# Turning phi_q into tiles of its own, and turning the last averages and the first dense rows with VectorE through DRAM

## The chip, the cores and the metric

The kernel runs on one core of a Trainium2 chip. A core has TensorE (PE, matrix products into PSUM), VectorE (DVE), ScalarE (ACT), GpSimd (POOL) and SyncE (SP), which here only issues transfers, in order; 16 DMA engines carry them. The metric is the device time of one execution in microseconds; the figure for the kernel before is the median of 3 runs.

## The reference

Two layers, each an attention block and a dense block with residuals. With x of shape 2048 x 640 and 32 heads of 20:

```python
def _A_ref(x, wqkv, w_phi, wo):
    q, k, v = qkv[0], qkv[1], qkv[2]
    pq = jnp.einsum("bhsd,hdf->bhsf", q, w_phi)
    pk = jnp.einsum("bhsd,hdf->bhsf", k, w_phi)
    phi_q = jnp.concatenate([_softmax(pq, axis=-1), _softmax(-pq, axis=-1)], axis=-1)
    phi_k = jnp.concatenate([_softmax(pk, axis=-1), _softmax(-pk, axis=-1)], axis=-1)
    kv = jnp.einsum("bhsf,bhsd->bhfd", phi_k, v)
    z  = jnp.einsum("bhsf->bhf", phi_k)
    num = jnp.einsum("bhqf,bhfd->bhqd", phi_q, kv)
    den = jnp.einsum("bhqf,bhf->bhq", phi_q, z)[..., None] + 1e-6
    o = num / den
    return (lambda x, *d: x.transpose(*d))(o, 0, 2, 1, 3).reshape(B, S, D) @ wo

def _B_ref(x, w1, b1, w2):
    h = jnp.einsum("bsd,df->bsf", x, w1) + b1
    sp = jnp.log1p(jnp.exp(-jnp.abs(h))) + jnp.where(h > 0, h, jnp.zeros_like(h))
    act = h * jnp.tanh(sp)
    return jnp.einsum("bsf,fd->bsd", act, w2)
```

Each is applied to a layer norm of x and added to x: attention, dense, attention, dense.

## The kernel before

The 2048 rows are 8 blocks (NB) of 256 rows, each two tiles (BT) of 128. Matrix products with the weights are done three times in a shortened float32, as high part times high part and the two mixed products, so most of PE's work comes in threes ("h" and "l" tiles). A product needs its left operand with the contracted dimension on the partitions: the class `Transposed` (L265) makes such a pair of high and low tiles, either from rows that PE turns (`rows`, the transposes at L280) or from tiles that are turned already (`cols`); ACT writes the high part and DVE the low part (L286).

A layer has three stages.

**First attention stage** (`attend_first`, L387). For each block there are six steps, k0, k1, v0, v1, q0, q1: a projection on PE (L344), then for keys and queries `features` (L355): copy, maximum and minimum, subtraction, exponential, sums and division, spread over ACT, DVE and POOL and over the following steps (`pending`, `advance`). Keys meet values in L416, which sums over all rows into `kva` and `kvz`. Query features (phi_q, 1280 columns: 32 heads x two softmaxes x 20) are turned by DVE in place in blocks of 32 x 32 (L425) and stored by four transfers per tile to `e_d` (L429), in runs of 32 numbers. The query tile, one of two, is free again when these have landed. Layer 0 fetches x (L384) and normalizes it here; layer 1 reads rows that the dense stage has turned and stored (`n2_d`, `load_turned` L319). Apart from a written-out SP order at the start, a scheduler lays out the engines' instructions here.

**Second attention stage** (`attend_second`, L553). The order of PE and SP is written out by hand. `load` (L521) brings the phi_q of a block back in two "big" tiles of five groups of 120 features and a small one; the tag "big" has 5 buffers, shared with the keys of the first stage and with dense temporaries. `average` (L563) multiplies the groups by the block-diagonal `kvb` (L573) and divides (L582 to L586) into row tiles, of which there are 4. In the loop over blocks (L637) the rows of the next block's averages are turned by PE (`Transposed(rows.pop(b + 1)).all()`, L658), while the block itself is projected by `o_ws` in halves (`Rows.half`, L600) and added to x (L603). `averages(b + 2)` (L660) and `phi(b + 4)` (L661) run for b from 2 to 5, so block 7's averages are made at b = 5. x has two buffers ("x"): each block is fetched one block ahead (L646) and stored (L669) at its end, so that a fetch waits for a store. Weights of the dense stage come in between (`fetches`, `makes`), and `tail` advances the last query tiles, which the first stage leaves over. At b = 5 `fetch_next` reads the first dense block's x1, at b = 6 `begin_next` normalizes it, and at b = 7 `ahead.all()` turns it on PE.

**Dense stage** (`dense`, L681). Per block six pairs of `hidden` (L695), `mish` and, two steps later, `contract` (L737). Rows of later blocks are normalized here, turned by DVE (`spill_turned`, L311) and stored to `n1_d` or, for the next layer, `n2_d`.

Of the kernel before, what the change touches and what calls it, by code (L numbers as in the profile page):

```python
# [24 lines left out]
BT = 2  # L25
# [17 lines left out]
def kernel(  # L43
# [36 lines left out]

    def row_block(t, b):
        return t[b * BLK:(b + 1) * BLK, :].rearrange("(p t) d -> p t d", t=BT)
# [182 lines left out]
    class Transposed:  # L265
# [5 lines left out]
        def step(self):  # L271
# [13 lines left out]
            act(hi, ps[:, :n], AF.Copy)  # L285
            nc.vector.tensor_tensor(lo, ps[:, :n], hi.bitcast(F32), op=ALU.subtract)  # L286
# [24 lines left out]
    def spill_turned(rows, dst):  # L311

        dst = dst.rearrange("(j f) (t q s) -> t q f j s", f=32, t=BT, s=32)
        for t in range(BT):
            nc.vector.transpose(rows[t], rows[t])
            for q in range(4):
                nc.sync.dma_start(dst[t, q], rows[t][32 * q:32 * q + 32].rearrange("f (j s) -> f j s", s=32))

    def load_turned(src, tiles):  # L319
# [6 lines left out]
        return Transposed(cols=cols)  # L326

# [59 lines left out]
    def attend_first(layer, x_src, first):  # L387


        def fetch_normed(b):  # L390
            if layer:
                return load_turned(n2_d[b], [row_tile] * 3)
            xt = fetch(x_src, b)
# [3 lines left out]
        pending = []  # L397

# [22 lines left out]
        def queries(xts, i, ps=None):  # L421
# [3 lines left out]
            nc.vector.transpose(e, e)  # L425
            b, t = divmod(i, BT)
            dst = e_d[b].rearrange("(j f) (t q s) -> t q f j s", f=32, t=BT, s=32)
            for q in range(4):
                nc.sync.dma_start(dst[t, q], e[32 * q:32 * q + 32].rearrange("f (j s) -> f j s", s=32))  # L429
                if b == NB - 1:  # L430
                    yield

# [88 lines left out]
    def load(b):  # L521

        ta, tb, tc_ = big_tile(), big_tile(), pair_tile(F32)
        for t, g0 in ((ta, 0), (tb, 5)):

            src = e_d[b][120 * g0:120 * (g0 + 4) + P]
            src = bass.AP(tensor=src.tensor, offset=src.offset, ap=[[BLK, P], [120 * BLK, 5], [1, BLK]])
            nc.sync.dma_start(t.rearrange("f (g s) -> f g s", s=BLK), src)
        nc.sync.dma_start(tc_[:80, 0], e_d[b][1200:])
        return [(ta, tb)[g // 5][:, (g % 5) * BLK:(g % 5 + 1) * BLK] for g in range(10)] + [tc_[:, 0]]  # L530

    def finish_kv(kva, kvz, mask):

        acc, acz = row_tile(), row_tile()
        for src, dst, p1, n, w in ((kva, acc, P, 4, 120), (kvz, acz, P, 1, 120), (kvz, acz, 42, 1, 80)):
            c = 120 if w == 80 else 0
# [362 lines left out]
```

## Time and profile before

| | |
|---|---|
| median of 3 runs | 1398.32 us (1397.06 to 1398.65) |
| the profiled execution | 1396.09 us |
| its span, first to last instruction | 1394.3 us |
| granted TensorE clock | 0.999 |
| first attention stage, layer 1 | 760 to 940 us, roughly |
| second attention stage, layer 1 | 945 to 1052 us |
| transfers | 169.57 MB in 350035 packets, 286866 of them under 512 B |
| stores of phi_q | 128 issues of 160 KB, 4.0 us to landing (median) |
| loads of phi_q | 32 of 640 KB (6.6 us) and 16 of 80 KB (6.3 us) |

In rows of groups the columns are line, engine, operation, output and input, shape, number, then busy us, mean ns of one, idle time of the engine before them and what ended it. In the timeline: start us, length us, engine, line, operation, number. In lists of waits: total us, times, longest.

### The profile page before, as it was taken

The page shows a single profiled execution, that of the slowest core. Times are in us where ns is not written, and L with a number is a line of the kernel's source. Part 1 is how long each engine was busy: PE and PEld are TensorE (multiplying, and loading weights), DVE is VectorE, ACT ScalarE, POOL GpSimd, SP SyncE. Part 2 cuts the span into 40 slices and gives each one's busy share as a digit, 9 for nine tenths or more (in the row PEclk, how much of TensorE's full clock was granted, in tenths as well). Part 3 has the DMA queues.
Part 4 walks back from the last instruction along what each step waited for, and adds up shares of the span by engine and source line. Part 5 has one row for each costly group of instructions (what it writes and reads, how often), then busy time and mean ns, then how long its engine had stood idle before and what let it go on. Part 6 is the DMA issues. An engine that isn't in the chain of part 4 may idle for free. (4 is left out here: it accounts for less than half of the span.)

```text
span 1394.3 us, 28137 instructions
## 1 busy us (share of the span) xinstructions
PE 1380.7 (99%) x11528; PEld 1367.0 (98%) x11528; DVE 1075.5 (77%) x1820; ACT 583.3 (42%) x973; POOL 440.0 (32%) x334
## 2 busy tenths in 40 slices
PE   7999999999999999999999999999999999999998
PEld 7999999999999999999999999999999999999998
DVE  5797877796698877788769988888767876777775
ACT  4444433321355454545454333332235444444443
POOL 1353443343422221222234434343342211211112
PEclk9999999999999999999999999999999999999999
DMA  8533333689633432343474333357976212333200
GB/s 328 162 79 54 67 52 58 184 228 307 235 86 95 114 84 62 83 114 95 122 261 87 71 57 58 65 107 231 288 257 200 76 25 72 95 95 95 75 22 20
DMA packets 350035, 169.57 MB, mean 122 GB/s; under 512 B 286866, under 2 KB 323458, under 8 KB 349906
## 3 DMA queue, kind: packets, MB, share of 16 engines
q1 hardware_dynamic: 349906, 167.78, 44.2%
q8 instruction: 90, 1.47, 0.4%
q14 instruction: 39, 0.32, 0.1%
HBM read 104.82 MB, written 62.91 MB: 120 GB/s over the span
## 5 line engine op out<-in xcount | busy, mean ns | idle before, releaser
L737 PE MATMUL mm<-r2h,ol 128*128 128x320 f32 x1280 | 304.7, 309 | 0.0
L721 POOL TENSOR_TENSOR ol<-big,ol 128x512 fp32r<-128x512 f32 (+1 forms) x98 | 129.8, 1324 | 483.5 <-ACT ol L720 407.3
L695 PE MATMUL one<-xtl,r1h 128*128 128x256 f32 x960 | 268.2, 279 | 0.0
L695 PE MATMUL one<-xth,r1l 128*128 128x256 f32 x960 | 268.0, 279 | 0.0
L695 PE MATMUL one<-xth,r1h 128*128 128x256 f32 x960 | 265.9, 279 | 0.0
L737 PEld LDWEIGHTS mm<-r2h,ol 128*128 128x128 f32 x1280 | 219.1, 188 | 0.0
L737 PE MATMUL mm<-r2l,ol 128*128 128x320 f32 x640 | 197.3, 309 | 0.0
L344 PE MATMUL mm<-r1h,xth 128*128 128x320 f32 x600 | 187.3, 312 | 0.0
L344 PE MATMUL mm<-r1h,xtl 128*128 128x320 f32 x600 | 186.0, 310 | 0.7 <-DVE xtl L286 0.7
L344 PE MATMUL mm<-r1l,xth 128*128 128x320 f32 x600 | 186.0, 310 | 0.0
L695 PEld LDWEIGHTS one<-xtl,r1h 128*128 128x128 f32 x960 | 180.4, 188 | 0.0
L695 PEld LDWEIGHTS one<-xth,r1l 128*128 128x128 f32 x960 | 180.4, 188 | 0.0
L695 PEld LDWEIGHTS one<-xth,r1h 128*128 128x128 f32 x960 | 179.6, 188 | 0.0
L710 DVE TENSOR_SCALAR big<-big 128x512 f32<-128x512 f32 (+1 forms) x98 | 57.1, 583 | 109.9 <-ACT big L708 109.7
L379 POOL TENSOR_TENSOR r<-r,r 128x1280 f32<-128x1280 f32 x32 | 75.8, 2368 | 163.1 <-DVE r L378 157.3
L737 PEld LDWEIGHTS mm<-r2l,ol 128*128 128x128 f32 x640 | 120.2, 188 | 0.0
L712 ACT ACTIVATE big<-big,two 128x512 f32<-128x512 f32 (+1 forms) x98 | 70.1, 715 | 116.2 <-DVE big L711 116.1
L708 ACT ACTIVATE big<-one,b1s 128x256 f32<-128x256 f32 x192 | 80.8, 467 | 90.1 <-PE one L695 89.6
L720 ACT ACTIVATE ol<-big 128x512 fp32r<-128x512 f32 (+1 forms) x98 | 61.0, 622 | 136.0 <-DVE big L719 135.9
L344 PEld LDWEIGHTS mm<-r1h,xth 128*128 128x128 f32 x600 | 112.8, 188 | 1.3
L344 PEld LDWEIGHTS mm<-r1h,xtl 128*128 128x128 f32 x600 | 112.7, 188 | 1.3 <-DVE xtl L286 1.0
L344 PEld LDWEIGHTS mm<-r1l,xth 128*128 128x128 f32 x600 | 112.8, 188 | 0.1
(129 smaller groups left out, 3156.1 us busy)
## 6 DMA issues: line engine op xcount, KB each, us to landing
e_d<-r SPq DMA_DIRECT2D x128, 160.0 KB, 4.0
big<-e_d SPq DMA_DIRECT2D x32, 640.0 KB, 6.6
x_d<-xt SPq DMA_DIRECT2D x23, 640.0 KB, 3.9
xt<-x_d SPq DMA_DIRECT2D x22, 640.0 KB, 4.3
n_d<-xn SPq DMA_DIRECT2D x176, 80.0 KB, 2.1
xt<-in_x SPq DMA_DIRECT2D x16, 640.0 KB, 5.9
xn<-x_d SPq DMA_DIRECT2D x28, 320.0 KB, 4.2
v<-n_d SPq DMA_DIRECT2D x30, 256.0 KB, 3.3
```

The source lines that it names most:

```text
L344: nc.tensor.matmul(ps[:, :HC], a[:, sl], r, start=(k == 0 and n == 0), stop=(k == KD - 1 and n == 2))
L379: nc.gpsimd.tensor_tensor(eg, eg, r.unsqueeze(2).to_broadcast([P, 2 * H, DH]), op=ALU.mult)
L695: nc.tensor.matmul(ph[:, j, :], l, r, start=(n == 0), stop=(n == 3 * KD - 1))
L708: exps[0] = nc.scalar.activation(part(ta, 0)[:, j - js.start], ph[:, j, :], AF.Exp, bias=b1s[:, 2 * pr + j:2 * pr + j + 1]).ins
L710: nc.vector.tensor_scalar_min(e, e, E_CAP)
L712: nc.scalar.activation(r, n, AF.Ln, bias=two)
L720: nc.scalar.activation(ah[:, js], n, AF.Copy)
L721: nc.gpsimd.tensor_tensor(al[:, js], n, ah[:, js].bitcast(F32), op=ALU.subtract)
L737: nc.tensor.matmul(pys[t][:, c, :HC], l[:, j, sl], r, start=(f == 0 and n == 0), stop=(f == KF - 1 and n == 2))
```

## The change

It has three parts, and a few adjustments that they need.

1. phi_q of blocks 0 to 6. DVE no longer turns a query tile in place: three transposes write two "big" tiles (groups 0 to 4 and 5 to 9, with an overlap) and a small one, which collect both tiles of a block. After the second tile twelve transfers store them to `e_d` and `f_d`, whose rows are as `load` wants them, so that `load` is three plain copies. Block 7 keeps the old way, through `g_d`. Since blocks of 32 x 32 end up in another order of rows, block rows are dealt to the tiles differently: layer 0 fetches a block of x in four transfers (`fetch_parts`), and the last dense stage's store of `n2_d` uses a permuted order (`first_stage`). The last group has 96 features, with zeros.
2. Averages of blocks 6 and 7. They are made at b = 3 and b = 4, a block sooner; DVE turns their rows (`turn_blocks`) into a "big" tile, eight transfers store it to `o_d` (`spill_blocks`) ahead of the block's x, and one transfer loads it back at b = 4 and b = 5 (`load_blocks`). PE does not turn these blocks any more.
3. The first dense block's rows. x1 is fetched at b = 4, normalized at b = 5, turned by DVE and stored to `n1_d`, and loaded at b = 6; at b = 7 only the high and low parts are made.

```diff
+    def row_parts(t, b):
+        return t[b * BLK:(b + 1) * BLK, :].rearrange("(h t s u) d -> u h s t d", h=2, t=BT, u=2)
...
-    e_d = [dram.tile([EW, BLK], F32, name=f"e_d{b}") for b in range(NB)]
+    e_d = [dram.tile([2, P, EW], F32, name=f"e_d{b}") for b in range(NB - 1)]
+    f_d = [dram.tile([96, BLK], F32, name=f"f_d{b}") for b in range(NB - 1)]
+    g_d = dram.tile([EW, BLK], F32, name="g_d")
+    o_d = [dram.tile([P, BT * D], F32, name=f"o_d{b}") for b in range(NB)]
...
+    def turn_blocks(o, t, dst):
+        nc.vector.transpose(dst[:, t * D:(t + 1) * D].rearrange("p (q c s) -> p q c s", q=4, c=KD),
+                            o.rearrange("p (c q f) -> p q c f", q=4, c=KD))
+
+    def spill_blocks(src, dst):
+        dst = dst.rearrange("(q f) (t k x) -> t k f q x", q=4, t=BT, k=4)
+        for t in range(BT):
+            for k in range(4):
+                nc.sync.dma_start(dst[t, k], src[32 * k:32 * k + 32, t * D:(t + 1) * D].rearrange("f (q x) -> f q x", q=4))
+
+    def load_blocks(src):
+        cols = big_tile()
+        nc.sync.dma_start(cols, src)
+        cols = cols.rearrange("p (a c s) -> p c a s", c=KD, s=32)
+        return Transposed(cols=[cols[:, c:min(c + 2, KD)] for c in range(0, KD, 2)])
...
+        def fetch_parts(b):
+            xt = x_tile()
+            for q in range(4):
+                nc.sync.dma_start(xt[32 * q:32 * q + 32], row_parts(x_src, b)[q // 2, q % 2])
+            return xt
...
-            nc.vector.transpose(e, e)
             b, t = divmod(i, BT)
-            dst = e_d[b].rearrange("(j f) (t q s) -> t q f j s", f=32, t=BT, s=32)
-            for q in range(4):
-                nc.sync.dma_start(dst[t, q], e[32 * q:32 * q + 32].rearrange("f (j s) -> f j s", s=32))
+            if b == NB - 1:
...
+            if t == 0:
+                blocks[b] = [big_tile(), big_tile(), pair_tile(F32).rearrange("p j s -> p (j s)")[:, :192]]
+            for c, dst in enumerate(blocks[b]):
+                src = e[:, EW - 96:].rearrange("p (j f) -> p j f", f=32)
+                if c < 2:
+                    src = e[:, 600 * c:600 * c + 600]
+                    src = bass.AP(tensor=src.tensor, offset=src.offset, ap=[src.ap[0], [32, 4], [120, 5], [1, 32]])
+                    dst = dst.rearrange("p (m g t s) -> p t m g s", m=4, t=BT, s=32)[:, t]
+                else:
+                    dst = dst.rearrange("p (j t s) -> p t j s", t=BT, s=32)[:, t]
+                nc.vector.transpose(dst, src)
+            if t == BT - 1:
+                for q in range(4):
+                    qs = slice(32 * q, 32 * q + 32)
+                    for c, (src, dst, m) in enumerate(zip(blocks[b], (e_d[b][0], e_d[b][1], f_d[b]), (4, 4, 3))):
+                        nc.sync.dma_start(dst.rearrange("(m f) (q x) -> q f m x", m=m, q=4)[q],
+                                          src[qs].rearrange("f (m x) -> f m x", m=m))
...
+            for c, t in enumerate((ta, tb)):
+                nc.sync.dma_start(t, e_d[b][c])
+            nc.sync.dma_start(tc_, f_d[b])
...
+                if b == NB - 2:
+                    ahead = load_next()
                 if b in (1, 2):
                     phi(b + 3)
-                if b == NB - 3:
+                if b == NB - 4:
                     fetch_next()
+                if b in (NB - 4, NB - 3):
+                    cols[b + 2] = load_blocks(o_d[b + 2])
                 r0.half(1, one_tile())
                 mv0 = r0.mean()
-                if b == NB - 2:
-                    ahead = begin_next()
+                if b == NB - 3:
+                    spill_next = begin_next()
...
-                    nxt = Transposed(rows.pop(b + 1)).all()
+                    nxt = (cols.pop(b + 1) if b + 1 in cols else Transposed(rows.pop(b + 1))).all()
                 if 2 <= b < NB - 2:
-                    averages(b + 2)
-                    phi(b + 4)
+                    if b < NB - 4:
+                        averages(b + 2)
+                        phi(b + 4)
+                    if b == NB - 4:
+                        turned = averages_turned(NB - 1)
                 if b == 2:
                     tail()
                 if b >= 2:
                     r1.half(0, one_tile())
+                if b == NB - 5:
+                    turned = averages_turned(NB - 2)
                 r1.half(1, one_tile())
                 norm_scale(b, [mv0, r1.mean()])
+                if turned is not None:
+                    spill_blocks(turned, o_d[b + 3])
+                    turned = None
+                if b == NB - 3:
+                    spill_next()
                 xt = xs.pop(b)
                 nc.sync.dma_start(row_block(x_dst, b), xt)
...
             def begin_dense():
-                return normed(0, x1t[0])
+                rows = [row_tile() for _ in range(BT)]
+                normalize(0, rows, [x1t[0][:, t, :] for t in range(BT)])
+                return lambda: spill_turned(rows, n1_d[0])
+
+            def load_dense():
+                return load_turned(n1_d[0], (v_tile, v_tile, row_tile))
```

More of the change, by code (lines that the diff above doesn't have):

```diff
@@ L397, in attend_first @@
         pending = []
+        blocks = {}
         def advance():
@@ L631, in averages, with averages_turned @@
                     average(b, t)
+            def averages_turned(b):
+                averages(b)
+                dst = big_tile()
+                for t, o in enumerate(rows.pop(b)):
+                    turn_blocks(o, t, dst)
+                return dst
             def phi(b):
```

58 lines of the change are left out of this document (35 added, 23 removed).

## The prediction

> **What bounds the kernel now.** I read the page's busy times first, then TensorE's (PE's) list of waits, then its timeline around the transposes, then VectorE's (DVE's) groups and stage windows, and last SyncE's (SP's) timeline, because the change moves most of its work there.
>
> ```profile
> PE 1380.7 (99%) x11528; PEld 1367.0 (98%) x11528; DVE 1075.5 (77%) x1820; ACT 583.3 (42%) x973; POOL 440.0 (32%) x334
> PE mm L237 <- DMA raw<-in_wqk_t: 7.1, 3, 4.1
> PE mm L573 <- PE mm L573: 0.9, 2, 0.4
> PE mm L344 <- DVE xtl L286: 0.7, 1, 0.7
> PE one L416 <- POOL big L379: 0.3, 1, 0.3
> ```
>
> PE is busy for 1380.7 of 1394.3 us. Of the 13.6 idle, 7.1 wait for the first weights, about 4.2 lie behind the last matmul, and everything in between is 1.9. So a microsecond of PE work taken out is a microsecond gained, as long as no new wait opens; nothing that other engines save counts.
>
> ```profile
> L280 PE MATMUL one<-ident,xn 128*128 128x128 f32 x260 | 37.2, 279 | 0.0
> 998.32 1.25 PE L280 MATMUL one<-ident,xn 128*128 128x128 f32 x10
> 999.50 1.39 PE L573 MATMUL mm<-kvb,big 120*64 120x63 f32 x40
> ```
>
> A mean of 279 ns is the length of one pipelined matmul. What a transpose occupies is the distance to the next start: ten begin at 998.32 and the next work at 999.50, so 1.18 us for ten, 118 ns each.
>
> **Removed from PE.** The turns of blocks 6 and 7 of the averages and of the first dense block's rows go: 3 x 10 transposes in each of 2 layers, 60 x 0.118 = **-7.1 us**. The averages themselves are only moved (two per block, 2.7 us); 96 in place of 80 contraction rows in the last group leaves the columns streamed as they were, so I count nothing, as for the one added small clear (0.06 us, by the row of the clear at L89) before the masks.
>
> **phi_q's turn on DVE (28 tiles).**
>
> ```profile
> L425 DVE STREAM_TRANSPOSE r<-r 128x1280 f32<-128x1280 f32 x32 | 47.7, 1490 | 3.6 <-POOL r L379 3.4
> L315 DVE STREAM_TRANSPOSE xn<-xn 128x640 f32<-128x640 f32 x44 | 36.3, 834 | 2.0 <-ACT xn L116 1.9
> L286 DVE TENSOR_TENSOR xtl<-xn,xth 128x512 fp32r<-128x512 f32 x14 | 16.6, 1188 | 0.0
> 197.20:226.30 29.10, 29.10 (x228) 28.77 (x227) 21.59 (x26) 11.83 (x17) 11.75 (x6) 1.00 0.28 42
> 864.30:893.40 29.10, 29.10 (x226) 28.79 (x225) 24.81 (x28) 10.53 (x15) 12.16 (x6) 1.00 0.36 60
> ```
>
> From the first two rows a turn costs (1490 - 834)/640 = 1.025 ns per column and 178 ns fixed. One instruction of 1280 columns becomes three of 640, 640 and 96: 834 + 834 + 276 = 1944 ns, +0.45 us per tile, +0.9 per block. No row shows a turn with strided blocks. Lower bound: if the fixed part is hidden, 1376 x 1.025 = 1.41 us, a gain of 0.08. Upper bound: the dearest DVE row per column, the third above, 2.32 ns, gives 3.19 us, +1.7 per tile. I take +0.45, since it is the same operation in runs of 32. The windows are one block of the first attention stage in each layer (total, PE, weight loads, DVE): DVE is busy 21.6 of 29.1 us in layer 0 and 24.8 in layer 1, so 4.3 us are free at the tightest and even the upper bound's 3.4 fits. Counted 0. If the cover were gone, each block would grow by what exceeds it. That e is now free after the turn and not after its store also takes away waits of ACT (37.5 us in all on e_d<-r), which PE never felt: 0.
>
> **SP and the transfers.** A block's phi_q is stored by 12 issues with runs of 1280 and 256 B, where there were 8 with runs of 128 B (median issue 0.65 us); by the 0.33 us of a 128-run load (L384) that is 4 us instead of 5. Its load has 128 runs of 5 KB per tile instead of 640 of 1 KB. SP has a gap of some 15 us in each block here (from 857.4 to 872.7, for one), so 0.
>
> **The head.** Block 0 of x comes in four transfers: SP's 0.43 us becomes 1.7, and the weights that PE awaits at 10.37 us (the last part of its 7.1) are issued 1.3 us later. Between 2.4 and 5.2 us the DMA engines were about 90% full, so bytes and not issue set the landing. Bounds 0 and 1.3; I take **+0.4**. The Trainium skill, "SBUF — State Buffer", section "Door 1: The DMA port swizzle", has 32 partitions reach 8 of 16 ports, 189 against 328 GB/s; were the four quarters run one after another, 655 KB would take 3.5 instead of 2.0 us, an estimate of +1.5 by which the sum would be 1.1 worse. Nothing here shows it: the four can run side by side.
>
> **The start of the second stage.** This is the one place where I expect a price. "big" has five buffers.
>
> ```profile
> 922.50 0.36 SPq L528 DMA_DIRECT2D big<-e_d  x1
> 943.84 0.38 SPq L528 DMA_DIRECT2D big<-e_d  x1
> 946.27 4.41 SPq L528 DMA_DIRECT2D big<-e_d  x2
> 942.40 2.54 PE L416 MATMUL one<-big,v 128*64 128x120 f32 x44
> 948.18 1.03 PE L573 MATMUL mm<-kvb,big 120*64 120x63 f32 x28
> ```
>
> Before, block 0's two tiles and one of block 1 were on their way by 922.5, and block 1's second went out at 943.84, for a first average at 948.18. After, block 6's phi_q holds two buffers from its first turn (929) until its 12 stores have landed (turned 938.5, 4 us of issue, 3 of landing: 946), and the last two key tiles hold two until L416 ends at 944.9. One buffer is left. If the loads take the free buffers first, as before, the turn waits instead, a 5 us delay that reaches PE hardly: 0. If not, three tiles of 640 KB go out from 945.5; with 2.1 us for the shortest landing in the DMA table and 0.36 MB/us (360 GB/s, as the later slices of this stretch show) the third lands at 953.1, or 954.5 by the longest landing here (8.5), against 951.5 wanted: 1.6 to 3 us. Bounds 0 and 3 per layer; I take 1.0, nearer to the early order that the trace shows: **+2.0** in two layers.
>
> **The moved averages and the way through DRAM.** I re-laid layer 1's timeline from 999.5 by the old pieces: a half of a row tile 2.2 us (60 matmuls for four in 8.8), a block's averages 2.7, ten transposes 1.2. Then averages 5 end at 1002.3, 6 at 1007.2, 7 at 1017.7; block 6 begins at 1030.9, 7 at 1039.7, dense at 1048.5. Block 6's average now starts 2.2 us after block 5's. DVE frees an accumulator pair in 0.173 + 0.153 + 0.352 + 0.657 + 0.315 = 1.65 us, and did so by 1002.7 and 1004.2; PE wants them at 1004.5 and 1005.8. Block 7's phi_q, loaded at 1008.39 (landing 5.3, so 1013.7 and a little), is wanted at 1015. Margins of 1 to 2 us, counted 0; without them up to 1 us each. The way back for block 7, from the average's end at 1017.7: DVE 1.65 + 2 x 0.83, 8 stores x 0.36, landing 2.1 to 4, load 4.3 to 6.6, split 2: about 1034 to 1036, wanted 1039.7. Block 6, by the same steps from 1007.2, has 5 us to spare. The dense rows: normalized 1029.4, turned 1031, 8 stores x 0.55 (L317's 4.37 for 8) to 1035.5; behind them on SP wait block 5's store and with it, two x buffers only, the fetch of x block 7 (store 3.2, fetch 4.3: landed at about 1043, wanted 1041.9, which delays DVE but finds four accumulators free), then the load: 1044, split by 1046, wanted by the first dense matmul at 1048.5. Counted 0, smallest margin 2.5 us.
>
> **Sum:** -7.1 + 0.4 + 2.0 = **-4.7 us**. Profiled execution 1396.09 (span 1394.3 and 1.8 around it) becomes 1391.4; its distance of 2.2 to the median of 1398.32 is kept: **1393.6**.
>
> **Rivals.**
> 1. *Late loads eat the gain.* The start of the second stage at its upper bound in both layers: -7.1 + 0.4 + 6 = -0.7, 1397.6. For it: DMA engines 88% busy from 943.5 to 956. Against it: longer runs load faster. Chance 0.17.
> 2. *Slower: DVE becomes the bound of the first attention stage.* From 1.49 + 4.3/2 = 3.6 us per tile the block outgrows PE in layer 1. At three times the row's rate (4.5 us) that is 0.86 us x 14 tiles = +12, giving 1406. For it: DVE's 85% there, overlapping and strided patterns that no row shows. Against it: the linear rows. Chance 0.11.
> 3. *The turned rows come back late.* If both legs land at 8.5 us as in the saturated stretch, block 7 is about 4 us late and the dense rows 3: 7 us in each layer, 1393.6 + 14 = 1407. For it: SP's fixed order, each store held until x can be replaced. Against it: at 1025 to 1038 landings were 3 to 4 us. Chance 0.08. The Trainium skill, "VectorE: DVE Perf Modes", section "Rules for kernel authors", says to turn 128x128 on TensorE where PSUM will do, since VectorE turns only 32x32 blocks: the rule speaks against this part, and the trace does price DVE's five blocks at 834 ns against PE's 590; but PE is the bound here, and DVE not.
>
> **Numbers.** Forecast 0.64, with a range of its own of 1390 to 1395.5; rivals 0.17, 0.11, 0.08. A measurement tells about 0.2%, 2.8 us, from no change: faster 0.64, same 0.17 (rival 1), slower 0.19 (rivals 2 and 3). The range runs from 1389.5 (all 7.1 kept, and most of the 1.9 of small waits) through rival 1 to 1403, leaving out most of rivals 2 and 3.
>
> **What would show it.** PE: L280's group at 200 instead of 260, and no new row among its waits but about 1 us per layer on the phi_q load. DVE: turns of 640 columns near 0.83 us; blocks of the first stage still 29.1 us long. A longer block there means rival 2; a wait of PE on xtl at the last two blocks or at the first dense matmul means rival 3; several us of wait at the first two averages, rival 1. I am wrong if the first stage's order shifts so that PE waits where it never did.

## The result, and the profile after

The changed kernel takes 1416.68 us (median of 4 runs, 1414.67 to 1417.5) beside 1398.20 for the kernel before (4 runs): a ratio of 1.0131, 95% interval 1.0114 to 1.0149. It is slower by 18.5 us where 4.7 us of gain were forecast. The profiled execution has a span of 1415.4 us after 1394.3.

The first line is that of busy time (page, part 1); then come PE's transposes and DVE's turns of phi_q among the groups of instructions (busy time, mean ns of one, idle time before them), and PE's waits (us in total, times, longest).

```profile
PE 1384.8 (98%) x11468; PEld 1366.3 (97%) x11468; DVE 1085.2 (77%) x1890; ACT 585.5 (41%) x973; POOL 447.2 (32%) x334
```

```profile
L290 PE MATMUL one<-ident,xn 128*128 128x128 f32 x200 | 29.7, 282 | 0.0
...
L479 DVE STREAM_TRANSPOSE big<-r 128x640 f32<-128x640 f32 x56 | 43.6, 815 | 5.0 <-POOL r L408 5.0
L479 DVE STREAM_TRANSPOSE ol<-r 128x96 f32<-128x96 f32 x28 | 6.5, 234 | 0.0
```

```profile
PE mm L247 <- DMA raw<-in_wqk_t: 10.9, 3, 4.2
PE one L452 <- POOL big L408: 4.8, 2, 2.8
PE one L779 <- DVE bn L666: 2.5, 1, 2.5
PE one L779 <- ACT xth L126: 2.2, 1, 2.2
PE mm L635 <- DMA big<-e_d: 1.5, 1, 1.5
...
PE mm L373 <- ACT xth L126: 0.9, 1, 0.9
```

The 60 transposes are gone, as forecast. In their place stand waits that PE did not have: on POOL at the last keys (L452), on the rows at the first dense matmul (L779), on a phi_q load (L635); the wait for the first weights grew from 7.1 to 10.9. Where each loss arises is read best by the start of the same matmul in both traces (a projection, an average or a dense matmul):

| stretch, up to | after - before there, us | lost in it |
|---|---|---|
| first projections (30 us) | +5.0 | 5.0 |
| first stage of layer 0, block 6 | +7.7 | 2.7 |
| averages of layer 0 running | +11.7 | 3.9 |
| dense stage of layer 0 running | +15.0 | 3.4, and the 3.5 saved: 6.9 |
| first stage of layer 1, block 6 | +14.6 | -0.4 |
| averages of layer 1 running | +19.1 | 4.5 |
| dense stage of layer 1, end | +21.0 | 1.9, and the 3.5 saved: 5.4 |

The products of keys and values of block 6 stand at +8.5 and +16.1, because the scheduler puts them later among the projections; that is order and no loss. In layer 1's first stage, then, nothing was lost. Of the 2.7 us in layer 0's, 1.4 fall around block 1, at the wait of 0.9 us on ACT; the other 1.3 fall ahead of it, and of the five kernels with the same order there (this one and the first four experiments) only this one and part 1 alone have such a loss (1.3 and 1.0).

Of the first 5.0 us some 1.5 belong to the profiled execution of before, which started quickly: the ten kernels below without part 1, whose block 0 is fetched as before, stand at +1.0 to +2.2 there (mean 1.5), the five with the fetch in four parts at +4.6 to +5.5 (mean 5.0).

**The head.** Block 0 of x landed at 8.8 us before, in one transfer, and at 11.62 after, in four quarters of 32 partitions.

**DVE's cover.** These windows (total, PE, weight loads, DVE, ACT, POOL, clock, DMA share, GB/s) lie around block 1 of each layer's first stage, of the kernel before and then of after:

```profile
71.50:89.00 17.50, 17.50 (x149) 16.87 (x148) 17.50 (x24) 9.03 (x14) 10.43 (x7) 1.00 0.37 81
753.70:768.80 15.10, 14.79 (x126) 14.28 (x125) 15.10 (x13) 6.78 (x11) 7.96 (x4) 1.00 0.39 67
```

```profile
78.00:95.50 17.50, 17.50 (x147) 16.78 (x145) 17.50 (x25) 6.85 (x10) 10.48 (x9) 1.00 0.51 119
767.90:784.90 17.00, 17.00 (x141) 16.39 (x140) 17.00 (x20) 6.00 (x9) 9.34 (x5) 1.00 0.46 107
```

DVE was busy for the whole of both windows before the change already. The blocks that I had read (from 197 and 864 us) are looser. Whether this is what cost the 1.4 us is settled below, by the run on VectorE's order.

**The order at the end of the first stage.** DVE in layer 1 before, and after:

```profile
936.65 1.51 DVE L425 STREAM_TRANSPOSE r<-r 128x1280 f32<-128x1280 f32 x1 [0.61 <-POOL r L379]
938.09 1.45 DVE L377 TENSOR_REDUCE r<-big 128x64 f32<-128x1280 f32 x1
939.57 0.55 DVE L378 RECIPROCAL r<-r 128x64 f32<-128x64 f32 x1
```

```profile
949.10 1.48 DVE L406 TENSOR_REDUCE r<-big 128x64 f32<-128x1280 f32 x1
950.50 0.95 DVE L407 RECIPROCAL r<-r 128x64 f32<-128x64 f32 x2
953.58 1.57 DVE L479 STREAM_TRANSPOSE big<-r 128x640 f32<-128x640 f32 x2 [2.13 <-POOL r L408]
955.08 0.23 DVE L479 STREAM_TRANSPOSE ol<-r 128x96 f32<-128x96 f32 x1
955.24 1.45 DVE L406 TENSOR_REDUCE r<-big 128x64 f32<-128x1280 f32 x1
956.60 1.53 DVE L397 TENSOR_REDUCE m<-r 128x32 f32<-128x640 f32 x2
958.05 0.54 DVE L407 RECIPROCAL r<-r 128x64 f32<-128x64 f32 x1
```

The last key's sum (L377, now L406) is followed at once by its reciprocal before; after, the queries' reductions (L397) stand between, and the query's own reciprocal had waited for a key's sum. POOL, which multiplies by that reciprocal, starts so much later that PE waits 2.8 us for it (2.0 in layer 0). The three turns of a tile take 2 x 815 + 234 ns = 1.86 us (groups above), so their size was forecast well; the scheduler's new order was not in the sum at all.

**The end of the second stage.** SP in layer 1 after (start, time of the group, count):

```profile
1027.72 6.28 SPq L349 DMA_DIRECT2D o_d<-big  x8
...
1040.20 6.83 SPq L349 DMA_DIRECT2D o_d<-big  x8
1047.12 0.38 SPq L753 DMA_DIRECT2D x_d<-xt  x1
...
1051.68 8.01 SPq L328 DMA_DIRECT2D n_d<-xn  x8
1059.78 0.49 SPq L753 DMA_DIRECT2D x_d<-xt  x1
...
1063.50 0.33 SPq L413 DMA_DIRECT2D xt<-x_d  x1
```

Eight stores take SP 6.3 to 8.0 us where I had counted 2.9 and 4.4. In the two groups to `o_d`, 2.4 and 3.1 us of that are waiting: an issue uses the semaphore of the transfer eight issues before it again and waits until that one has landed. A store of 1031.29 went out when a phi_q load landed at 1031.28, one of 1046.72 when the load of turned rows landed at 1046.71. In the group to `n_d` only 0.3 us lie between the issues; two of the eight take 1.8 and 2.8 us themselves, and no view says why. The trace of before had such issues in a full stretch of its own, which I had not priced: four stores of phi_q in layer 1 with 0.05 us between them.

```profile
981.03 6.89 SPq L429 DMA_DIRECT2D e_d<-r  x4
```

After the change the store of x stands behind the stores of turned rows (1059.78), the fetch into its buffer behind that store (1063.50), and the load of the dense rows behind the fetch (1063.99). x is there at 1069.45 and the first dense rows at 1070.08, so block 7's residual and the split of the dense rows are late together, and PE behind both:

```profile
1067.92 0.30 PE L373 MATMUL one<-r2h,xtl 128*128 128x320 f32 x1
1070.76 0.76 PE L779 MATMUL one<-xth,r1h 128*128 128x256 f32 x2 [2.54 <-DVE bn L666]
...
1072.16 0.41 PE L779 MATMUL one<-xth,r1l 128*128 128x256 f32 x1
1072.37 0.41 PE L779 MATMUL one<-xth,r1h 128*128 128x256 f32 x1
```

The wait is followed by matmuls that start 0.21 us apart, where they start 0.117 us apart otherwise. The granted clock (third figure from the end) is 0.50 there for 3.4 us, as it is behind the wait at layer 0's first dense matmul and behind layer 1's wait on POOL, and 1.00 elsewhere behind the head:

```profile
388.16:391.57 3.41, 3.36 (x15) 3.06 (x16) 3.34 (x9) 1.51 (x3) 0.62 (x2) 0.50 1.03 411
961.60:965.01 3.41, 3.41 (x25) 3.20 (x22) 1.22 (x4) 1.27 (x1) 0.00 (x0) 0.50 0.72 258
1070.83:1074.24 3.41, 3.16 (x13) 2.86 (x14) 3.38 (x9) 1.60 (x3) 0.52 (x2) 0.50 1.04 405
```

So each of these three waits costs about 1.7 us, half of 3.4, more than its length: some 5 us of the loss.

### The profile page after: what moved, and what is told of

Its sections match the earlier page's. It is cut to its first block, busy times and chain, and to the rows that moved or that the text cites. A ratio compares the mean times of both kernels' runs of the same rounds, so it can differ in the third digit from the quotient of the medians.

```text
span 1415.4 us, 28221 instructions
## 1 busy us (share of the span) xinstructions
PE 1384.8 (98%) x11468; PEld 1366.3 (97%) x11468; DVE 1085.2 (77%) x1890; ACT 585.5 (41%) x973; POOL 447.2 (32%) x334
## 4 chain that ended last, share of the span: by engine, by line
PE 84%; DMA 6%; DVE 5%; issue 2%; ACT 1%; SPq 1%; POOL 1%; DVEq 0%; ACTq 0%; POOLq 0%
PE mm L373 25%; PE mm L821 23%; PE one L779 22%; PE one L373 7%; PE mm L635 2%; PE one L452 2%; PE one L290 1%; DMA big<-o_d 1%; DVE xtl L297 1%; DMA raw<-in_wqk_t 1%; DMA xt<-in_x 1%; DMA big<-x_d 1%; DMA big<-in_wv 1%; DMA x_d<-xt 1%; DMA xn<-in_w 0%
## 5 line engine op out<-in xcount | busy, mean ns | idle before, releaser
L779 PE MATMUL one<-xth,r1h 128*128 128x256 f32 x960 | 267.4, 281 | 4.7 <-DVE bn L666 2.5
L779 PE MATMUL one<-xtl,r1h 128*128 128x256 f32 x960 | 269.6, 281 | 0.3 <-DVE xtl L297 0.3
L779 PE MATMUL one<-xth,r1l 128*128 128x256 f32 x960 | 269.0, 280 | 0.0
L779 PEld LDWEIGHTS one<-xth,r1h 128*128 128x128 f32 x960 | 180.9, 189 | 5.4 <-ACT xth L126 5.4
L779 PEld LDWEIGHTS one<-xtl,r1h 128*128 128x128 f32 x960 | 181.7, 189 | 0.9 <-DVE xtl L297 0.9
L779 PEld LDWEIGHTS one<-xth,r1l 128*128 128x128 f32 x960 | 181.7, 189 | 0.0
```

The source lines that it names most:

```text
L779: nc.tensor.matmul(ph[:, j, :], l, r, start=(n == 0), stop=(n == 3 * KD - 1))
```

## The experiments

Times are medians beside runs of the kernel before in the same job (1397.9 to 1398.9); intervals are 95%.

**The head: one transfer.** Which rows stand in which partition changes, so the output's rows are mixed.

```diff
-            xt = x_tile()
-            for q in range(4):
-                nc.sync.dma_start(xt[32 * q:32 * q + 32], row_parts(x_src, b)[q // 2, q % 2])
-            return xt
+            return fetch(x_src, b)
```

> The changed kernel, but layer 0 fetches a block of x in one transfer of plain rows instead of four (rows of layer 0 then stand in another order than the stores assume, so the output's rows are mixed). The trace of the changed kernel puts 5 us of its loss before the first projections (30.0 to 35.1 us) and 3.3 more in the rest of layer 0's first stage. Theory (the four transfers cost it, by whatever mechanism): the first weights arrive at 10.4 again instead of 14.4, PE's waits on them go from 10.9 back to about 7.1, and the time falls by 6 to 8 us, to about 1409. Rival (the turn of phi_q on DVE and the new order cost it, the transfers only seem to): at most 2 us less, 1415 or more.

1413.77 us, ratio 1.0107 (1.0092 to 1.0122); x landed at 9.44, the first projections stand at +0.7 instead of +5.0, and 2.9 us of the median come back, between the theory's 6 to 8 and the rival's 2. The head is a cost of part 1.

**The head: four transfers of columns.** Four quarters of the columns, each over all 128 partitions (rows mixed as well).

```diff
-                nc.sync.dma_start(xt[32 * q:32 * q + 32], row_parts(x_src, b)[q // 2, q % 2])
+                cs = slice(160 * q, 160 * q + 160)
+                nc.sync.dma_start(xt[:, :, cs], row_block(x_src, b)[:, :, cs])
```

> As the run with plain x, again with rows in another order than the stores assume, but the block comes in four transfers of a quarter of the columns, each over all 128 partitions. Same bytes, same number of transfers as in the changed kernel, all partitions in each. Theory A (number: SP issues a transfer only when the one eight before it has landed, so three more transfers push the weights behind landings): the weights arrive late as in the changed kernel, PE waits 10 to 11 us for them, time within 2 us of 1416.7. Theory B (32 partitions are slow for a transfer): as with plain x, waits of 7 to 8 us, time near 1409.

x landed at 10.06 us. In the twelve kernels that fetch it in one transfer it landed between 8.8 and 10.04, in the five with quarters of 32 partitions between 11.62 and 12.41. So the number of transfers is not told from the spread, and the 32 partitions cost 1.6 us or more: the landing goes by theory B. The first projections stand at +2.4, between 0.7 and 5.0. The median (1417.63, ratio 1.0125, 1.0105 to 1.0144) doesn't show this saving.

**The store of x first.** At the end of a block of the second stage:

```diff
                 norm_scale(b, [mv0, r1.mean()])
+                xt = xs.pop(b)
+                nc.sync.dma_start(row_block(x_dst, b), xt)
...
                     spill_next()
-                xt = xs.pop(b)
-                nc.sync.dma_start(row_block(x_dst, b), xt)
```

> The changed kernel with each block's store of x ahead of the stores of turned rows on SP, at b = 3, 4 and 5. Theory (the way round SP is the price at the end of the second stage: turned rows' stores, then the store of x, then the fetch of x that DVE needs, then the load of the dense rows): stores of x go out 6 to 8 us sooner, x of block 7 lands before DVE wants it, PE's waits on the first dense matmul (2.3 and 2.7 us) shrink below 1, and the time falls by 3 to 6 us, to about 1412. Rival (the turned dense rows themselves are late, whatever the order): the waits stay or grow, since the turned rows are stored later; 1416 or more.

1420.42 us, 1.0153 (1.0129 to 1.0177). In the profile, that of the fastest execution (1415.62), the waits stay: 2.2 us at layer 1's first dense matmul on DVE bn, and in layer 0 2.0 on block 7's turned rows (ACT xth), which now come back late. My theory, that the order alone did it, fell: what stood ahead of the one stands ahead of the other.

**Part 1 alone** (phi_q in tiles of its own, x in four parts; averages and dense rows as before).

> Part 1 of the change alone: phi_q in tiles of its own with the four-part fetch of x; averages and first dense rows turned by PE as before. Theory (part 1 costs by itself: head 5, first stage of layer 0 3.3, start of the second stage 3.2 and 3.1, layer 1 1.0; parts 2 and 3 give 7.1 on PE and lose 12 at the ends of the second stages): 15 us over the kernel before, 1413 to 1414, the first dense matmul without a wait. Rival (the parts need each other: the loss at the second stage's start comes from the buffers that parts 2 and 3 hold): under 1408.

1413.54 us, 1.0113 (1.0083 to 1.0143), as its theory had it. +5.5 at the first projections, +7.8 at the end of layer 0's first stage, 3.7 and 4.5 lost at the two second stages' starts (the waits on POOL, and behind each of them 3.4 us at a granted clock of 0.50, from 278.18 and 957.43), nothing at the dense starts.

```profile
PE mm L247 <- DMA raw<-in_wqk_t: 11.4, 5, 5.0
PE one L452 <- POOL big L408: 4.8, 2, 2.8
```

**Parts 2 and 3 without part 1.** The kernel before with the moved averages, the turned blocks and the dense rows of the change; phi_q (L425, L429, L528) and x as before.

> Part 1 undone, parts 2 and 3 kept: phi_q turned in place and loaded as in the kernel before, block 6's and 7's averages and the first dense rows turned through DRAM. Theory (the loss of 12 us at the ends of the second stages is theirs alone, from 4 MB more to move per layer in a stretch whose DMA engines are full): no loss up to the first averages, then -3.5 per layer by the transposes and +5 to +7 per layer around the first dense matmul; +3 to +5 over the kernel before, 1401 to 1404, with PE waiting 2 us and more at the first dense matmul. Rival (phi_q's part crowds them, they are right by themselves): the transposes' 7 us show, 1392.

1407.78 us, 1.0073 (1.0058 to 1.0088), dearer than expected. Nothing is lost ahead of the averages; the ends of the second stages lose about 7.8 and 7.1 us, 3.5 saved in each. So both halves of the change are slower by themselves, for different reasons.

```profile
PE one L737 <- ACT xth L117: 2.4, 2, 2.0
PE one L364 <- DVE xt L623: 1.8, 2, 1.1
PE one L364 <- ACT xth L117: 1.3, 2, 0.7
PE one L737 <- DVE bn L624: 1.3, 1, 1.3
```

**Part 2 alone, part 3 alone.**

> Part 2 alone on the kernel before: averages of blocks 6 and 7 a block sooner, turned by DVE and through DRAM. It saves 40 transposes, 4.7 us. Theory (bytes in a full stretch): 2.6 MB more per layer delay the weights and x, waits of 1 to 2 us per layer at the last blocks; 1395 to 1398, near the kernel before. Rival (the first dense rows, part 3, are what is late): 1393.5.

> Part 3 alone on the kernel before: the first dense block's rows normalized a block sooner, turned by DVE, stored and loaded. It saves 20 transposes, 2.4 us. Theory (bytes in a full stretch): 1.3 MB more per layer and a chain of store, fetch of x and load that ends at the first dense matmul; waits of 1 to 3 us per layer there, 1397 to 1401. Rival (part 2 is the dear one): 1396.

1409.50 (1.0090, 1.0074 to 1.0105) and 1408.74 (1.0083, 1.0065 to 1.0102): either is as dear as both together and dearer than both of its theories, so their prices don't add. The clock has a share in that: in the profiled executions it is 0.50 for 6.8 us in each layer with part 2 alone, for 3.4 and 6.8 us with part 3 alone, and for 3.4 us in all with both. With part 3 alone, PE waits where block 7's rows are turned, for the residual sum that waits for x:

```profile
PE one L280 <- DVE xt L603: 6.9, 5, 3.4
```

**VectorE's order.** After, with the queries' reductions (L397) and the sums (L406) tied behind the previous tile's reciprocal:

```diff
+    last_recip = [None]
...
-        for s, op in ((0, ALU.max), (1, ALU.min)):
-            nc.vector.tensor_reduce(m[:, s], eh[:, 1], axis=AX.X, op=op)
+        with ExitStack() as st:
+            if last_recip[0] is not None:
+                st.enter_context(tc.issue_after(last_recip[0]))
+            for s, op in ((0, ALU.max), (1, ALU.min)):
+                nc.vector.tensor_reduce(m[:, s], eh[:, 1], axis=AX.X, op=op)
...
-        nc.vector.tensor_reduce(r, eg, axis=AX.X, op=ALU.add)
-        nc.vector.reciprocal(r, r)
+        with ExitStack() as st:
+            if last_recip[0] is not None:
+                st.enter_context(tc.issue_after(last_recip[0]))
+            nc.vector.tensor_reduce(r, eg, axis=AX.X, op=ALU.add)
+            last_recip[0] = nc.vector.reciprocal(r, r).ins
```

> The changed kernel with DVE's order in the first stage tied: the maximum, minimum and sum of a tile come no sooner than the reciprocal of the tile before. In the changed kernel's trace the reciprocal of the last query tile but two comes after a key's sum and the last key's reciprocal after two query reductions, and PE waits 2.2 and 2.9 us for GpSimd's product with it, 4 us and more per layer at the start of the second stage. Theory (the order that the scheduler laid out costs this): those waits shrink below 1 us and 4 to 7 us come back, 1410 to 1412. Rival (DVE's added work and GpSimd's lateness cost it, in any order): the waits stay, 1415 or more.

1410.13 us, 1.0094 (1.0069 to 1.012): 6.5 us come back and the waits on POOL are gone, so the order was a cause. It was also the cause of the loss around block 1 of layer 0: the five kernels with part 1 and the scheduler's order lose 1.4 to 2.0 us there, this run 0.1 (+4.6 at the first projections, +4.7 at block 6), although it makes the same three turns per tile and DVE is as full:

```profile
74.00:94.00 20.00, 20.00 (x164) 19.17 (x165) 20.00 (x28) 10.34 (x16) 13.64 (x9) 1.00 0.45 104
```

What had been hidden behind the order shows:

```profile
PE mm L642 <- DMA big<-e_d: 4.3, 3, 2.3
PE one L786 <- ACT xth L127: 3.8, 3, 2.0
```

The first are the late phi_q loads: with what follows the second stages' starts lose 3.9 us in layer 0, 1.7 of them at half clock, and 1.9 in layer 1.

**Block 6 alone through DRAM**, on the kernel before: of part 2 only what concerns `averages_turned(NB - 2)`; averages 7 stay at their old place.

```diff
-                    averages(b + 2)
-                    phi(b + 4)
+                    if b != NB - 4:
+                        averages(b + 2)
+                        phi(b + 4)
```

> One half of part 2 alone, on the kernel before: only block 6 of the averages is made a block sooner and turned through DRAM (8 stores and 1 load, 1.3 MB per layer); block 7 and the dense rows are turned by TensorE as before, phi_q and the head are as before. 20 transposes go: 20 x 0.118 = 2.4 us. Theory 'the end of the stage is what is full' (eight transfers in flight, the fetch of x block 7 behind the stores there): these 8 stores go out about 1008 to 1018, long before, and block 6 had 5 us to spare, so the gain is kept but for 0.5 us per layer: 1395 to 1397.5, waits of TensorE on xt or on split rows below 1 us. Theory 'every way through DRAM in the second stage is dear' (both blocks lost about 16 us in two layers, so half of that each): 1398.3 - 2.4 + 8 = 1404, with 2 to 4 us of wait per layer.

1401.79 us, 1.0033 (1.002 to 1.0046), over a wide spread (1398.37 to 1407.8). The 2.4 us saved aren't kept, and the theory that only the very end is full fell; the rival, at 1404, is nearer.

**Fewer transfers.** Parts 2 and 3, with four stores per turned block, and the dense rows turned into one "big" buffer too:

```diff
-        dst = dst.rearrange("(q f) (t k x) -> t k f q x", q=4, t=BT, k=4)
-        for t in range(BT):
-            for k in range(4):
-                nc.sync.dma_start(dst[t, k], src[32 * k:32 * k + 32, t * D:(t + 1) * D].rearrange("f (q x) -> f q x", q=4))
+        dst = dst.rearrange("(q f) (t k x) -> k f t q x", q=4, t=BT, k=4)
+        for k in range(4):
+            nc.sync.dma_start(dst[k], src[32 * k:32 * k + 32].rearrange("f (t q x) -> f t q x", t=BT, q=4))
...
-                return lambda: spill_turned(rows, n1_d[0])
+                flat = big_tile()
+                for t, o in enumerate(rows):
+                    turn_blocks(o, t, flat)
+                return lambda: spill_blocks(flat, n_d)
...
-                return load_turned(n1_d[0], (v_tile, v_tile, row_tile))
+                return load_blocks(n_d)
```

> Parts 2 and 3 as in the run without part 1, with the same bytes in fewer transfers: each turned block is stored by 4 issues in place of 8 (both row tiles in one transfer), and the first dense rows go the same way into one buffer (4 stores and 1 load in place of 8 and 3). 13 issues per layer at the end of the stage where there were 24 stores and 3 loads became 12 stores and 3 loads. Theory 'number' (each issue waits for the transfer eight before it, so the count of transfers sets when the fetch of x block 7 goes out): that fetch goes out some 5 us sooner, the loss per layer falls from about 7.8 to 3 or less, 1397 to 1402, and the 8 stores that took 6.3 to 8 us of SP become 4 that take under 4. Theory 'bytes' (4 MB more in a stretch whose transfers were already 0.68 to 0.99 busy): nothing changes by more than 2 us, 1406 to 1410, and 4 stores take as long as 8 did.

1401.17 us, 1.0021 (1.0013 to 1.003): 6.6 us less than with eight stores. SP in layer 1 with eight stores and with four:

```profile
1029.89 8.06 SPq L340 DMA_DIRECT2D o_d<-big  x8
...
1042.58 7.99 SPq L319 DMA_DIRECT2D n_d<-xn  x8
...
1054.40 0.33 SPq L404 DMA_DIRECT2D xt<-x_d  x1
```

```profile
1025.57 3.29 SPq L340 DMA_DIRECT2D o_d<-big  x4
...
1038.52 2.93 SPq L340 DMA_DIRECT2D n_d<-big  x4
...
1047.18 0.33 SPq L404 DMA_DIRECT2D xt<-x_d  x1
1047.67 0.33 SPq L344 DMA_DIRECT2D big<-n_d  x1
```

With four, issues of 0.58 to 1.05 us follow one another without a wait. With eight, 4.4 us of the first 8.06 are waiting for older transfers, and of the second 7.99 one issue takes 2.8 itself. The fetch of x goes out 7.2 us sooner, 3.6 of which the run with eight stores had lost before this point. The bytes are the same, so bytes are not what came back. (The dense rows also come back in one load of longer runs here; that share isn't told apart from the number.)

**The load first.** As the run with fewer transfers, and

```diff
+                if b == NB - 2:
+                    ahead = load_next()
                 if b + 1 < NB:
                     xs[b + 1] = fetch(x_src, b + 1)
-                if b == NB - 2:
-                    ahead = load_next()
```

> As the run with fewer transfers, but SyncE issues the load of the first dense rows ahead of the fetch of x block 7 instead of behind it. In that run the stores of these rows had landed at 1045.56, but the load stood behind the fetch, which waits for block 5's store of x to land and went out at 1047.18; the load followed at 1047.67 and TensorE waited about 2 us for its split at the first dense matmul, in both layers, with the clock at 0.91 for some time after. Theory 'SP's order holds the load': it goes out at about 1045.7, 2 us sooner, the wait at the first dense matmul falls below 0.5 us, and with the clock's loss after it about 2.5 us per layer come back: 1396 to 1397.5, faster than before by about 0.1%. Theory 'bytes': the load lands at the same time as before, since it shares the DMA engines with seven others, and the time stays at 1400 to 1402; or the fetch of x block 7 is now late and the wait moves to the last rows' transposes.

1398.69 us, 1.0001 (0.9992 to 1.001): about half of what was expected. The load went out at 1045.54, and PE's waits on the split dense rows (1.8 us in layer 0, 0.7 in layer 1) are gone; in their place it waits there on xt, 1.2 and 0.5 us, and 1.0 us on block 7's split rows. The expectation had misread the run that it starts from: in layer 1 that wait was 0.7 us and not 2, and the granted clock behind it was 1.00.

**The whole change with these three mended** (order, number, load first).

> The whole change (part 1 too) with three of its causes taken away: VectorE's order tied as in the run on order (6.5 us), 4 stores per turned block and the dense rows in one buffer (6.6 us in the run without part 1), and the load of these rows ahead of the fetch of x block 7 (4 us if that holds). If the causes add up: 1416.7 - 6.5 - 6.6 - 4 = 1399.6, so 1398 to 1402; what stays is the head (5), layer 0's first stage (3.3) and the late phi_q loads at both second stages' starts (2 to 4 each), against 7.1 saved. If instead block phi_q's stores and loads press on the same transfers, the second stage's end stays 3 us per layer worse than without part 1 and the time is 1403 to 1408.

1405.73 us, 1.0054 (1.0042 to 1.0066): 11 of the 17 us. The head stays (+5.4), and so do the late phi_q loads (2.8 us on big<-e_d; the starts of the second stages lose 3.5 and 3.1), and the ends of the second stages still lose 3.5 and 4.7 us. Layer 0's first stage, which the expectation had counted among what stays, loses nothing (+5.5 at block 6).

**Which way pays?** The run with the load first without block 7's part (the same edit of `averages` as for block 6 alone), and block 6 alone with four stores.

> As the run with the load first, but block 7 of the averages is turned by TensorE as before and averaged at its old place: block 6 and the first dense rows go through DRAM (4 stores and 1 load each). 40 transposes go: 40 x 0.118 = 4.7 us. In the run with the load first all three ways broke even, 7.1 saved and as much lost, and its waits stood at block 7: 1.5 us for phi_q's last load (needed a block sooner), 1.0 us for the split of its turned rows, 1.4 for the fetch of x block 7. Theory 'block 7 is the way that doesn't pay': its own 2.4 us cost 4 or more, and without it the time is 1395 to 1397 with waits below 1.5 us per layer. Rival 'what is lost goes with any transfers at the end of the stage': the dense rows' 4 stores alone still hold the fetch of x block 7, the waits stay at 2 to 3 us per layer and the time at 1398 to 1400.

> Only block 6 of the averages through DRAM, with 4 stores in place of 8 (the run with block 6 alone gave 1401.8, over a wide spread of 1398.4 to 1407.8). 20 transposes go, 2.4 us. If the count of transfers is what that run lost by, 1395.5 to 1397.5 and a spread as narrow as before's; if not, 1400 to 1402 again.

1402.42 (1.0028, 1.0018 to 1.0038) and 1401.68 (1.0021, 1.0012 to 1.0031): without block 7 both of its theories fell, and for block 6 alone the rival held: its number of stores isn't what it lost by. Fewer ways cost more than all three (1398.69), and in both PE waits for xt (6.1 and 2.0 us).

**x block 7 in a buffer of its own.** The two runs "load first" and "block 6, four stores", each with

```diff
-                    xs[b + 1] = fetch(x_src, b + 1)
+                    spare = big_tile().rearrange("p (t d) -> p t d", t=BT) if b == NB - 2 else None
+                    xs[b + 1] = fetch(x_src, b + 1, spare)
```

and in the first this fetch again ahead of the load.

> As the run with the load first, but x block 7 is fetched into a buffer of 'big' that is free by then, not into one of the two x buffers, and its fetch stands ahead of the load of the dense rows again. So it no longer waits until block 5's store of x has landed. Theory 'chain through two x buffers': add, store of x, landing, fetch two blocks on, landing, add; in the kernel before one round of it took 9.0 us (store issued 343.74, landed 347.31, fetch landed 352.79), with the turned rows' transfers ahead of it the store alone takes 7 to 10 us to land, and what TensorE saves is waited for at xt. Without it the fetch lands before 1043 in layer 1, TensorE's waits on xt go (1.7 us and the clock's loss behind them), and what is left of the 7.1 us is some 3 us: 1394 to 1396.5. Rival 'the transfers as such': the fetch takes its share of the DMA engines sooner and the turned rows land later by as much; waits on split rows of 1 to 2 us per layer in place of those on xt, 1397.5 to 1400.

> Block 6 alone through DRAM with 4 stores, and x block 7 in a buffer of 'big' of its own. By the theory of the chain through two x buffers the waits on xt go (1.0 and 1.0 us in layer 0, and what follows them), and the 2.4 us are kept: 1395.5 to 1397. If the transfers as such cost more than they save, 1400 to 1402 as in the run without it.

The first gave 1396.67 us, 0.9983 (0.9974 to 0.9991): **faster than both kernels**, 2.2 us of median below the kernel before. It has parts 2 and 3 without part 1. From the run with fewer transfers (1401.17) it differs by that buffer alone. Its waits in PE's list are those of the head and little else; the first four:

```profile
PE mm L239 <- DMA raw<-in_wqk_t: 8.2, 3, 4.7
PE mm L593 <- DMA big<-e_d: 1.3, 2, 1.1
PE mm L593 <- PE mm L593: 0.9, 2, 0.4
PE one L364 <- ACT xth L118: 0.8, 2, 0.6
```

The second stayed at 1402.07 (1.002, 1.001 to 1.0031) with 2.0 us on xt. Its trace shows the same chain one block sooner: block 4's store of x, issued at 1024.91 behind two loads, landed at 1034.67, and block 6's fetch went out at 1034.74. In layer 0 the same store took 9.0 us to land (346.18 to 355.21), and before 3.6 (343.74 to 347.31). In the run with all three ways block 7's averages stand ahead of that point and give x time; that this is why three ways go where one doesn't is read from the traces, not tried.

## Why the prediction was wrong

- **PE's saving of 7.1 us** was right: 200 transposes instead of 260. That a microsecond off PE is gained "as long as no new wait opens" held as well; the condition failed.
- **phi_q's turn**: forecast 1.94 us per tile, measured 1.86, right. Its cover was misread: "4.3 us are free at the tightest" holds for the windows from 197 and 864 us, and around block 1 nothing was free, before the change already. But that isn't what cost: with the order tied the same turns cost PE 0.1 us there, with DVE just as full. "Counted 0" came out right for the turns themselves.
- **The order of the first stage** was taken as given, a term at nothing without a reason. A scheduler lays it out, and part 1 changed it (the waits on POOL are there with part 1 alone; which of its pieces turned the order was not tried): tying it gave back 6.5 us of median. In the trace it was 2.0 and 2.8 us of waits on POOL, 1.7 of half clock behind the second and 1.4 around block 1; waits that had been hidden behind these took part of it back. The prediction's last sentence named it as a way to be wrong, without a price.
- **The head**: +0.4, bounds 0 and 1.3; 5.0 in the profile, 3.6 against the mean of the other heads. "Bytes and not issue set the landing" left out the partitions. The Trainium skill, "SBUF — State Buffer", section "Door 1: The DMA port swizzle", by which 32 partitions reach half the ports, gave an estimate of +1.5. The direction agrees; the two landings of four transfers, 10.06 over 128 partitions and 11.62 over 32, put 1.6 us on the partitions.
- **The start of the second stage**: +2.0, bounds 0 and 6 for both layers. In the whole change most of it was hidden behind the order; once that was mended, 3.9 + 1.9 = 5.8 us, the upper bound, 1.7 of it by the clock. Rival 1 was right in kind. Its "longer runs load faster" didn't show: 640 KB of phi_q took 7.3 us to land in runs of 5 KB (median of 28) and 6.6 in runs of 1 KB (32), amid more other transfers.
- **SP and the way through DRAM**, counted 0 with a smallest margin of 2.5 us: the dearest miss, 6.9 + 5.4 us. The step that failed is "8 stores x 0.36" and "8 stores x 0.55": durations from stretches where nothing stood in the way. In this one SP needs 6.3 to 8.0 us for eight, partly waiting for transfers eight issues older (2.4 and 3.1 us), partly in issues that take up to 2.8 us themselves; that pushes the store of x, and with two buffers the fetch. Landings of 2.1 to 4 us came from the old stretch, with DMA engines 0.74 busy from 1000 to 1044; the change made it 0.94 from 1020 to 1064, with stores of the turned rows landing 2 to 7 us after their issue and loads after 5 to 7.
- **The clock** was not in the sum: every wait was priced at its length, and three of them cost 1.7 us more.
- **Rival 3** (1407, chance 0.08) described this, with "each store held until x can be replaced" as its reason. Parts 2 and 3 by themselves gave 1407.78; that the numbers meet is partly luck, since the rival's 1407 holds 2.4 us for part 1. Its chance was too small.
- **The Trainium skill**, "VectorE: DVE Perf Modes", section "Rules for kernel authors", says to turn 128x128 on TensorE. I set it aside because PE is the bound. The runs bear the rule out for this change, though not by the turn's price: it is the way through memory that costs. With that mended, turning on DVE is worth 0.17%.
- **The range** to 1403 took the rivals as alternatives. Order, head and late rows came true at once, and the range held no sum of them.

## What to carry to other kernels

Cost a new transfer by the stretch that it is put into: how many transfers stand ahead of it in its queue, what each waits for, and which buffer's next fetch waits behind it. Merging transfers of the same bytes gave 6.6 us here, and one more buffer for x turned parts 2 and 3 from even to a gain. Look for cover in the tightest block, and where a scheduler lays out the order, count on the order changing. Price a wait of PE at more than its length where the clock can fall behind it.

## What the hardware showed that was not expected

After waits of 2.2, 2.8 and 2.5 us the granted clock fell to 0.50 for 3.41 us each time; behind the first and the third, where dense matmuls follow, those of 256 columns started 0.213 us apart instead of 0.117. The three falls begin 573.44 and 109.23 us apart, which is 168 and 32 times 3.413: they lie on a grid of their own length. That fits a wait that was not followed by one. The wait on POOL that ended at 276.62 had 2.0 us, but a line of that grid (275.52) cuts it in two; with part 1 alone the same wait lay within one piece of its run's grid, and the clock fell from 278.18. How much of a piece has to be idle was not tried.

The Trainium skill, "TensorE: Matmul & The Clock Gate", section "What's actually happening", has PE fall to half clock after an idle window of about 3.4 us; half clock agrees with the 0.213 (256 columns at 1.2 GHz), but here waits of 2.2 to 2.8 us were enough.

The spread goes with the clock as well. Block 6 alone went from 1398.4 to 1407.8 where the kernel before stays within 3 us: its fastest execution, the profiled one, has a mean granted clock of 1.000, the six others (1401.0 to 1407.8) 0.997 or 0.998. That in these a margin of a microsecond was missed and the clock fell behind the wait is a guess; they were not profiled.

What stays open: of the 7.1 us the best version keeps some 2.2; its remaining waits were read, not removed. Why some issues of stores take 2 to 3 us is open, and so is which piece of part 1 turned the scheduler's order.
